# Second score pass of the later heads as 64-row products in the two halves of TensorE's rows

## The chip, the cores and the metric

The kernel runs on one core of a Trainium2 chip, as one program. The metric is the device time of one execution in microseconds (us), the median of several runs. Before the change it is 1375.22 us over 3 runs (1374.31 to 1378.02).

## The reference, cut to what matters

```python
scores = scale * np.matmul(q, k.transpose(0, 1, 3, 2))      # q, k, v: 4 x 12 x 448 x 64, f32
scores = cap * np.tanh(scores / cap)
scores = scores - np.max(scores, axis=-1, keepdims=True)
attn = np.exp(scores)
attn = attn / (np.sum(attn, axis=-1, keepdims=True) + 1e-09)
x = matmul(attn, v), heads side by side                      # 4 x 448 x 768
xn = (x - mu) / np.sqrt(var + 1e-06) * g_ln
x = x + np.maximum(xn @ w_ch1, 0.0) @ w_ch2                  # 768 -> 3072 -> 768
h = np.maximum(x.transpose(0, 2, 1) @ w_tok1, 0.0) @ w_tok2  # 448 -> 256 -> 448
u = x + h.transpose(0, 2, 1)
out = u + np.maximum(u @ w_ch1b, 0.0) @ w_ch2b               # 768 -> 1536 -> 768
```

Four batches, twelve heads each, head dimension 64. All inputs are f32.

## The kernel before, in words

**Data.** Activations lie transposed: channels on the 128 partitions, the 448 tokens along the free dimension. A product of TensorE here is one matmul instruction with a moving operand of 448 columns, and nearly all of them are made in fp32r, one pass over the columns. To keep f32 precision each operand x is split in two fp32r numbers: `high` is a rounded copy of x, `low` is x minus `high` (the helper `low`, L172, a subtraction). A product of two split operands is then made of high by high, high by low and low by high, the small low by low is left out (`PASSES`).

**Stages.** Batches 0 and 1 (`early`) come first: their attention works in plain f32, since TensorE has nothing else to do then. Their layer norm and the first MLP (`mlp`, L587 and L608, groups of four 128-wide hidden tiles), the token mixing (`tokens`) and the second MLP follow. The attention of batches 2 and 3 (the later heads, 24 of them) is woven in between the MLP products of batches 0 and 1. Then batches 2 and 3 go through the same MLPs and the token mixing, with no attention left to weave.

**Order of the work.** The program writes steps with `add(engine, cols, run, reads, writes, early)`; a step has a key (where in the program it belongs, minus `early`) and a cost, and `Program.emit` plays all steps through a list of engines: at each turn the engine that is free first takes the ready step with the lowest key. The instructions then stand on each engine in that fixed order. A step given as "dve+/pool+" goes to VectorE or GpSimd, whichever the planner finds free; steps marked + share one port in the planner, so that two of them do not overlap there. "act/dve*+" is a choice of ScalarE or VectorE.

**A later head.** Two DMAs bring q and k into `qk` and v into `v`. In `qk` the 64 rows of q and of k lie twice, in partitions 0 to 63 and again in 64 to 127 (`heads` in the launch code). Four steps prepare the scores: ScalarE writes `ks` (128x512), the high part of k in all 128 partitions (L347); a subtraction on GpSimd or VectorE overwrites partitions 64 to 127 of it with the low part (L348, recorded at L172), so that `ks` is [high; low]; and `qs` gets the high part of q in column block 0 and the low part in column block 1, both in all 128 partitions (L349, L350). There is one `ks` and one `qs` buffer, so they are written anew for a head when the scores of the head before are done.

The step `scores` (L358 to L366) makes for each half of a head two of its four blocks of 128 keys:

```python
for i in range(2):
    c, rows = 2 * half + i, slice(i * D, (i + 1) * D)
    ...
    for j in range(2):
        mm(sc.at[:, i, :S], ks.at[:, c * P:(c + 1) * P], qs.at[:, j], start=j == 0, stop=j == 1)
```

With j = 0 the 128 rows give (high k + low k) times high q, with j = 1 (high k + low k) times low q. So a half takes four products of 128 rows, a head eight, and the 24 later heads 192 in 48 halves. The two blocks of a half go to two PSUM banks (`sc.at[:, 0]` and `sc.at[:, 1]`).

The early heads (L363) take f32 operands: 64 rows of k and q, block i from the i-th half of the partitions. A product in f32 shows in the trace as two matmul records.

Behind the scores of a head stand tanh and exp on ScalarE (L369, L370), the row maxima and sums on VectorE (L374, L421), the split of the exponentials into `eh` and `el` (L394, L172, L400), the value products (L408) and the write into x (L429, L430).

Of the kernel before, what the change touches and what calls it, by code (L numbers as in the profile page):

```python
# [18 lines left out]
B, H, S, D = 4, 12, 448, 64  # L19
C = H * D  # L20
P = 128
# [38 lines left out]
URGENT, SCORES, PREPARE, LOAD = 1000.0, 19.31, 4.58, 24.58  # L60
# [26 lines left out]
class Program:  # L87
# [11 lines left out]
    def add(self, engine, cols, run, reads=(), writes=(), early=0.0):  # L99

        names = [(name.strip("*+"), "*" in name, "+" in name) for name in engine.split("/")]
        costs = {e: self.FIXED[e] + self.RATE[e] * cols * (0.5 if half else 1.0) for e, half, _ in names}
        step = Step(costs, run, (self.key - early, len(self.steps)))
        step.port = {e for e, _, port in names if port}
        before = set()
        for b in [p for b in reads for p in b.parts]:
            before.add(b.writer)
            b.readers.append(step)  # L110
        for b in [p for b in writes for p in b.parts]:
            before.add(b.writer)
            before.update(b.readers)
            b.writer, b.readers = step, []
        before -= {None, step}
        for s in before:
            s.users.append(step)
        step.waits = len(before)
        self.steps.append(step)
# [32 lines left out]
def block_kernel(ctx: ExitStack, tc: tile.TileContext, qkv, cap, gln, w1, w2, wt1, wt2, con, out):  # L152
    nc = tc.nc
    mm, act, dve = nc.tensor.matmul, nc.scalar.activation, nc.vector
    engine_of = {"dve": nc.vector, "pool": nc.gpsimd}
    prog = Program()
    add = prog.add
# [13 lines left out]
    def low(eng, out, whole, high):  # L171
        eng.tensor_tensor(out, whole, high.bitcast(F32), op=ALU.subtract)  # L172

    def copy(e, out, a):
        if e == "act":
            act(out, a, AF.Copy)  # L176
        else:
            dve.tensor_copy(out, a)
# [27 lines left out]
    def area(n):  # L206
        ends.append(ends[-1] + n)
        return area_t[:, ends[-2]:ends[-1]]
# [6 lines left out]
    two = [Box(area(S)), Box(area(S))]  # L215
# [113 lines left out]
    def attention(b, start, pace):  # L329
        x = x_t[b]  # L330
        early, beside = b < 2, b in BESIDE
# [5 lines left out]
        def head(h):  # L337
            grp = h // 6
            pr, hh = divmod(h, 2)
            qk, v, m = next(qks), next(vls), next(ms)  # L340
            add("dma", 480, lambda: nc.sync.dma_start(out=qk.at, in_=qkv[b, h, :, :S + 4 * P]), (), [qk], early=LOAD)
            add("dma", 192, lambda: nc.sync.dma_start(out=v.at, in_=qkv[b, h, :, S + 4 * P:].rearrange("p (c d) -> p c d", c=4)), (), [v], early=LOAD)
            q, k = qk.at[:, :S], qk.at[:, S:]
            if not early:

                (ks,), (qs,), (vs,), (eh,), (el,) = KS, QS, VS, EH, EL
                add("act", 4 * P, lambda: act(ks.at, k, AF.Copy), [qk], [ks], early=PREPARE)  # L347
                add("dve+/pool+", 4 * P, lambda e: low(engine_of[e], ks.at[D:], k[D:], ks.at[D:]), [qk], [ks], early=PREPARE)  # L348
                add("act/dve*+", S, lambda e: copy(e, qs.at[:, 0], q), [qk], [qs], early=PREPARE)  # L349
                add("dve+/pool+", S, lambda e: low(engine_of[e], qs.at[:, 1], q, qs.at[:, 0]), [qk], [qs], early=PREPARE)  # L350

            E = []
            for half in range(2):
                sc, eb = next(scs), next(es)
                e, eb = eb.at, [eb]
                E.append((e, eb))

                def scores(half=half, sc=sc):  # L358
                    for i in range(2):
                        c, rows = 2 * half + i, slice(i * D, (i + 1) * D)  # L360
                        if early:

                            mm(sc.at[:, i, :S], k[rows, c * P:(c + 1) * P], q[rows], start=True, stop=True)  # L363
                        else:
                            for j in range(2):
                                mm(sc.at[:, i, :S], ks.at[:, c * P:(c + 1) * P], qs.at[:, j], start=j == 0, stop=j == 1)  # L366

                add("pe", (6 if early else 4) * S, scores, [qk] if early else [ks, qs], [sc], early=URGENT + SCORES)
                add("act", 2 * S, lambda e=e, sc=sc: act(e, sc.at[:, :, :S], AF.Tanh, scale=tsc), [sc], eb)  # L369
                add("act", 2 * S, lambda e=e: act(e, e, AF.Exp, scale=cap_t), (), eb)  # L370

            for half in range(2):
                e, eb = E[half]
# [13 lines left out]
            else:  # L387
# [4 lines left out]
                for half in range(2):  # L392
                    e, eb = E[half]
# [23 lines left out]
            if beside:  # L417
                other, n = Box(E[1][0][:, 1], E[1][1]), next(sums)
                for half in range(2):
                    e, eb = E[half]  # L420
# [50 lines left out]
        for h in range(H):  # L471
            prog.key = start + h * pace
            head(h)
            if h % 6 == 5:
                prog.key = start + (h + 1) * pace
                divide(h // 6)
# [325 lines left out]
```

## Time and profile before

| | |
|---|---|
| median of 3 runs | 1375.22 us (1374.31 to 1378.02) |
| the profiled execution, first to last instruction (its span; nothing is recorded around it) | 4738.7 us |
| instructions in its trace | 17824, of them 6468 matmuls and 6468 weight loads |
| TensorE matmuls busy (PE) | 4729.0 us, 100% of the span |
| VectorE (DVE) busy | 897.2 us, 19% |
| ScalarE (ACT) busy | 624.6 us, 13% |
| GpSimd (POOL) busy | 88.9 us, 2% |
| DMA | 281.04 MB, 59 GB/s over the span |

The profiled execution took 3.45 times as long as the timed runs. So a duration of TensorE in the profile is not its duration in a timed run, and the shares of the other engines in the span are much smaller than their shares in a timed run must be. PE is TensorE's matmuls, PEld its weight loads, which may run beside matmuls. Line numbers such as L366 are those of the kernel before; the changed kernel's stand 3 or 4 higher behind the change.

### The profile page before, as it was taken

To read this page: it belongs to the slowest core of one execution; us is meant where nothing else is said; L and a number is where in the kernel's file an instruction comes from. 1 tells how busy PE (TensorE), PEld (TensorE's weight loads), DVE (VectorE), ACT (ScalarE), POOL (GpSimd) and SP (SyncE) were. 2 spreads that over 40 slices of the span, in tenths; PEclk is the share of its full clock that TensorE was granted. 3 is DMA by queue.
4 is the path that set the end of the run, shared out by engine and by line. 5 is a ranking of instruction groups with operands and counts; after the bars stand their busy time and mean duration, and the time that the engine had idled before them with its cause. 6 is when DMAs were issued, how large, how long until landed. Compare 5 with 4: busy or idle time off the path is not lost.

```text
span 4738.7 us, 17824 instructions
## 1 busy us (share of the span) xinstructions
PE 4729.0 (100%) x6468; PEld 2684.3 (57%) x6468; DVE 897.2 (19%) x1612; ACT 624.6 (13%) x1006; POOL 88.9 (2%) x79
## 2 busy tenths in 40 slices
PE   9999999999999999999999999999999999999999
PEld 2223555555655556665555555555656555656555
DVE  2231222222222222222222221100000000000000
ACT  3321111211121111121111110000000000000000
POOL 1100000000000000000000000000000000000000
DMA  3221122111212111221111211111111111111111
GB/s 105 97 66 39 46 69 67 59 61 64 67 55 67 63 57 41 67 65 61 60 60 51 72 57 53 57 62 58 53 53 44 61 59 60 51 47 42 37 57 58
DMA packets 147095, 281.04 MB, mean 59 GB/s; under 512 B 10816, under 2 KB 79680, under 8 KB 147008
## 3 DMA queue, kind: packets, MB, share of 16 engines
q1 hardware_dynamic: 146432, 279.62, 18.5%
q8 instruction: 51, 0.84, 0.1%
q10 hardware_dynamic: 576, 0.29, 0.0%
q14 instruction: 36, 0.29, 0.0%
HBM read 217.74 MB, written 62.13 MB: 59 GB/s over the span
## 4 chain that ended last, share of the span: by engine, by line
PE 100%; DMA 0%; ACT 0%; DVE 0%; issue 0%
PE bank L587 39%; PE bank L608 39%; PE bank L384 6%; PE sc L363 3%; PE sc L366 3%; PE bank L408 3%; PE bank L663 2%; PE bank L685 2%; PE bank L639 1%; PE bank L466 1%; PE bank L531 0%; PE bank L495 0%; PE bank L511 0%; DMA area<-in_qkv 0%; PE bank L445 0%; PE bank L444 0%
## 5 line engine op out<-in xcount | busy, mean ns | idle before, releaser
L587 PE MATMUL bank<-big,split 128*128 128x448 f32 x2592 | 1898.7, 995 | 1.1 <-ACT big L543 1.1
L608 PE MATMUL bank<-h,split 128*128 128x448 f32 x2592 | 1896.3, 995 | 0.0
L587 PEld LDWEIGHTS bank<-big,split 128*128 128x128 f32 x2592 | 1109.4, 429 | 750.5 <-issue 740.4
L608 PEld LDWEIGHTS bank<-h,split 128*128 128x128 f32 x2592 | 1109.5, 428 | 744.9 <-issue 741.6
L612 DVE TENSOR_TENSOR x<-x,bank 128x448 f32<-128x448 f32 x216 | 134.1, 621 | 1407.4 <-PE bank L608 1407.4
L592 ACT ACTIVATE h<-bank 128x448 fp32r<-128x448 f32 x144 | 78.4, 545 | 1817.5 <-PE bank L587 1817.5
L593 DVE SCALAR_TENSOR_TENSOR h<-bank,h 128x448 fp32r<-128x448 f32 x144 | 89.9, 624 | 1182.2 <-ACT h L592 1182.1
L366 PE MATMUL sc<-qs,ks 128*128 128x448 f32 x192 | 151.5, 994 | 0.0
L384 PE MATMUL bank<-x,area 128*96 128x448 f32 (+1 forms) x88 | 129.3, 1665 | 0.0
L363 PE MATMUL sc<-area 64*128 64x448 f32 x112 | 112.0, 1695 | 5.0 <-DMA area<-in_qkv 5.0
L366 PEld LDWEIGHTS sc<-qs,ks 128*128 128x128 f32 x192 | 82.5, 431 | 57.6 <-issue 57.2
L384 PE MATMUL bank<-x,x 128*96 128x448 f32 (+1 forms) x76 | 112.5, 1675 | 0.0
L685 PE MATMUL bank<-t,h 128*128 128x448 f32 x144 | 108.3, 996 | 0.0
L176 ACT ACTIVATE split<-whole 128x384 fp32r<-128x384 f32 (+1 forms) x96 | 54.0, 564 | 340.2 <-PE bank L608 228.7
L276 ACT ACTIVATE whole<-raw 128x384 f32<-128x384 f32 (+2 forms) x130 | 76.7, 593 | 125.5 <-DVE split L172 107.8
L663 PE MATMUL bank<-big,t 128*128 128x384 f32 x136 | 89.8, 899 | 0.0
L172 DVE TENSOR_TENSOR split<-whole,split 128x384 fp32r<-128x384 f32 (+1 forms) x112 | 68.9, 619 | 108.1 <-ACT split L176 107.7
L408 PE MATMUL bank<-el,vs 128*128 128x448 f32 x96 | 88.6, 989 | 0.0
L685 PEld LDWEIGHTS bank<-t,h 128*128 128x128 f32 x144 | 61.4, 427 | 40.8 <-issue 40.0
L384 PEld LDWEIGHTS bank<-x,area 128*96 128x96 f32 (+1 forms) x88 | 28.5, 347 | 95.4 <-issue 85.5
L279 DVE SCALAR_TENSOR_TENSOR whole<-raw,whole 128x384 int32<-128x384 int32 (+2 forms) x130 | 79.8, 616 | 0.2
L363 PE MATMUL sc<-x 64*128 64x448 f32 x80 | 79.4, 1692 | 0.0
(112 smaller groups left out, 1719.0 us busy)
## 6 DMA issues: line engine op xcount, KB each, us to landing
split<-kept SPq DMA_DIRECT2D x160, 384.0 KB, 3.4
split<-kept SPq DMA_DIRECT2D x120, 512.0 KB, 3.6
raw<-in_w SPq DMA_DIRECT2D x72, 384.0 KB, 3.3
kept<-split SPq DMA_DIRECT2D x72, 384.0 KB, 3.0
raw<-in_w SPq DMA_DIRECT2D x54, 512.0 KB, 3.6
kept<-split SPq DMA_DIRECT2D x54, 512.0 KB, 3.3
area<-in_qkv SPq DMA_DIRECT2D x38, 480.0 KB, 3.5
area<-in_qkv SPq DMA_DIRECT2D x35, 192.0 KB, 2.4
```

What stands on the lines that cost most here:

```text
L279: add("dve+", m, lambda: dve.scalar_tensor_tensor(f, hi, -(1 << 31), f, op0=ALU.bitwise_and, op1=ALU.bitwise_or), [r], [w])
L363: mm(sc.at[:, i, :S], k[rows, c * P:(c + 1) * P], q[rows], start=True, stop=True)
L366: mm(sc.at[:, i, :S], ks.at[:, c * P:(c + 1) * P], qs.at[:, j], start=j == 0, stop=j == 1)
L384: mm(po.at[:DV, :S], v.at[:n, c], E[c // 2][0][:n, c % 2], start=c == 0, stop=c == 3)
L408: mm(po.at[:, :S], vs.at[:, c, :P], part.at[:, i], start=c == 0 and part is eh, stop=c == 3)
L587: mm(ph.at[:, :S], w[:, wi, cc * P:(cc + 1) * P], src[cc].at[:, xi], start=(cc, n) == (0, 0), stop=(cc, n) == (NCC - 1, 2))
L592: add("act", S, lambda ht=ht, ph=ph: act(ht.at[:, 0], ph.at[:, :S], AF.Relu), [ph], [ht], early=EVACUATE)
L593: add("dve", S, lambda ht=ht, ph=ph: dve.scalar_tensor_tensor(ht.at[:, 1], ph.at[:, :S], 0.0, ht.at[:, 0].bitcast(F32), op0=ALU.max, op1=A ...
L608: mm(py.at[:, :S], w[:, wi, i * P:(i + 1) * P], h[i].at[:, hi], start=(i, n) == (0, 0), stop=(i, n) == (G - 1, 2))
L612: add("dve", S, lambda x=x, py=py: dve.tensor_tensor(x.at, x.at, py.at[:, :S], op=ALU.add), [py], [x], early=EVACUATE)
L663: mm(pj.at[:, :CC], t1[:, wi, sc * DT + j * P:sc * DT + (j + 1) * P], cols(xs[sc])[:, xi], start=(sc, wi, xi) == (0, 0, 0), stop=(sc, wi) ...
L685: mm(pu.at[:, :S], hT[j].at[:, hi, a:a + P], t2[:, wi, j * S:(j + 1) * S], start=(j, n) == (0, 0), stop=(j, n) == (1, 2))
```

## The change

For the later heads the low part of k is now laid out by key block. In the even blocks (0 and 2) it lies in partitions 64 to 127 as before, in the odd blocks (1 and 3) in partitions 0 to 63, and the high part in the other half. That takes two subtractions of 64 x (2x128) instead of one of 64x512. The first pass, all 128 rows of both blocks times high q, is unchanged in what it computes. The second pass takes only the 64 rows that hold high k, times the same 64 rows of low q: rows 0 to 63 for the half's first block, rows 64 to 127 for its second. The product low k by low q is thereby left out. The first pass of both blocks comes first, then the second pass of both. The planner's cost of a later half goes from 4 to 3 products of 448 columns.

```diff
@@ -345,7 +345,10 @@
 
                 (ks,), (qs,), (vs,), (eh,), (el,) = KS, QS, VS, EH, EL
                 add("act", 4 * P, lambda: act(ks.at, k, AF.Copy), [qk], [ks], early=PREPARE)
-                add("dve+/pool+", 4 * P, lambda e: low(engine_of[e], ks.at[D:], k[D:], ks.at[D:]), [qk], [ks], early=PREPARE)
+                for odd in range(2):
+                    lows = slice((1 - odd) * D, (2 - odd) * D)
+                    kl, kw = (t[lows].rearrange("p (a two c) -> p a two c", two=2, c=P)[:, :, odd] for t in (ks.at, k))
+                    add("dve+/pool+", 2 * P, lambda e, kl=kl, kw=kw: low(engine_of[e], kl, kw, kl), [qk], [ks], early=PREPARE)
                 add("act/dve*+", S, lambda e: copy(e, qs.at[:, 0], q), [qk], [qs], early=PREPARE)
                 add("dve+/pool+", S, lambda e: low(engine_of[e], qs.at[:, 1], q, qs.at[:, 0]), [qk], [qs], early=PREPARE)
 
@@ -356,16 +359,17 @@
                 E.append((e, eb))
 
                 def scores(half=half, sc=sc):
-                    for i in range(2):
-                        c, rows = 2 * half + i, slice(i * D, (i + 1) * D)
+                    blocks = [(i, slice((2 * half + i) * P, (2 * half + i + 1) * P), slice(i * D, (i + 1) * D)) for i in range(2)]
+                    if not early:
+                        for i, c, _ in blocks:
+                            mm(sc.at[:, i, :S], ks.at[:, c], qs.at[:, 0], start=True, stop=False)
+                    for i, c, rows in blocks:
                         if early:
-
-                            mm(sc.at[:, i, :S], k[rows, c * P:(c + 1) * P], q[rows], start=True, stop=True)
+                            mm(sc.at[:, i, :S], k[rows, c], q[rows], start=True, stop=True)
                         else:
-                            for j in range(2):
-                                mm(sc.at[:, i, :S], ks.at[:, c * P:(c + 1) * P], qs.at[:, j], start=j == 0, stop=j == 1)
-
-                add("pe", (6 if early else 4) * S, scores, [qk] if early else [ks, qs], [sc], early=URGENT + SCORES)
+                            mm(sc.at[:, i, :S], ks.at[rows, c], qs.at[rows, 1], start=False, stop=True)
+
+                add("pe", (6 if early else 3) * S, scores, [qk] if early else [ks, qs], [sc], early=URGENT + SCORES)
                 add("act", 2 * S, lambda e=e, sc=sc: act(e, sc.at[:, :, :S], AF.Tanh, scale=tsc), [sc], eb)
                 add("act", 2 * S, lambda e=e: act(e, e, AF.Exp, scale=cap_t), (), eb)
```

`sc` and the tiles are those of before, `P` is 128, `S` 448, `D` 64.

The order on TensorE (PE) at the first later head, batch 2's head 0, whose two halves write `sc_115` and `sc_116`; the neighbours are value products of the early heads. Before:

```order
L384 MATMUL bank_111<-x_82,x_83 96x448 x4
L366 MATMUL sc_115<-qs_95,ks_96 128x448 x4
L366 MATMUL sc_116<-qs_95,ks_96 128x448 x4
L384 MATMUL bank_112<-x_82,x_83 96x448 x2
L384 MATMUL bank_112<-x_83 96x448 x2
```

And now:

```order
L388 MATMUL bank_111<-x_82,x_83 96x448 x4
L365 MATMUL sc_115<-qs_95,ks_96 128x448 x2
L370 MATMUL sc_115<-qs_95,ks_96 128x448 x2
L365 MATMUL sc_116<-qs_95,ks_96 128x448 x2
L370 MATMUL sc_116<-qs_95,ks_96 128x448 x2
L388 MATMUL bank_112<-x_82,x_83 96x448 x2
L388 MATMUL bank_112<-x_83 96x448 x2
```

Each half's four products have become two of one line and two of another, with nothing between; here the halves stand at the same place.

The order on GpSimd (POOL) from its last weight subtraction on; `ks` is the low part of k, `qs` that of q. Before:

```order
L172 TENSOR_TENSOR split_79<-whole_75,split_79 128x512
L280 TENSOR_TENSOR whole_76<-whole_76,raw_73 128x512
L172 TENSOR_TENSOR split_77<-whole_76,split_77 128x512
L172 TENSOR_TENSOR ks_96<-area,ks_96 64x512
L172 TENSOR_TENSOR qs_95<-area,qs_95 128x448
```

And now:

```order
L172 TENSOR_TENSOR split_79<-whole_75,split_79 128x512
L280 TENSOR_TENSOR whole_76<-whole_76,raw_73 128x512
L172 TENSOR_TENSOR split_77<-whole_76,split_77 128x512
L172 TENSOR_TENSOR ks_96<-area,ks_96 64x2x128 x5
L172 TENSOR_TENSOR qs_95<-area,qs_95 128x448
```

Each subtraction on `ks` has become two. Counted over the whole listing, GpSimd has 46 of the 48 halves (22 of 24 whole ones before) and 22 of `qs` (23 before); VectorE has 2 halves of `ks` (2 whole ones before), 2 of `qs` (1 before), 2 casts of `qs` (4 before) and 40 casts of `split` (30 before), which ScalarE has lost. GpSimd goes from 84 to 107 instructions, VectorE from 1614 to 1623, ScalarE from 1012 to 1004; TensorE and the DMA issues keep their number.

The order on TensorE in the middle of batch 2's heads, where a group of the first MLP of batches 0 and 1 (`big_84` and `big_85`) begins: L587's products with weight buffers `split_77`, `split_78` and `split_79` follow one another. Before, from `split_78` on:

```order
L587 MATMUL bank_114<-big_84,split_78 128x448 x18
L587 MATMUL bank_112<-big_85,split_78 128x448 x6
L366 MATMUL sc_115<-qs_95,ks_96 128x448 x4
L408 MATMUL bank_111<-eh_98,vs_97 128x448
L408 MATMUL bank_111<-el_99,vs_97 128x448 x2
L587 MATMUL bank_112<-big_85,split_78 128x448 x12
L587 MATMUL bank_113<-big_84,split_79 128x448 x18
```

And now, from `split_77` on:

```order
L591 MATMUL bank_112<-big_84,split_77 128x448 x18
L365 MATMUL sc_116<-qs_95,ks_96 128x448 x2
L370 MATMUL sc_116<-qs_95,ks_96 128x448 x2
L591 MATMUL bank_113<-big_85,split_77 128x448 x18
L591 MATMUL bank_114<-big_84,split_78 128x448 x18
L591 MATMUL bank_112<-big_85,split_78 128x448 x18
L591 MATMUL bank_113<-big_84,split_79 128x448 x12
```

Inside the products with `split_78` stood the 21st of the 48 score halves; now none stands there, and ahead of them, among those with `split_77`, it is the 18th. Counted over the listing, the first two halves have 42 products of the MLPs and the token mixing ahead of them in both kernels, the 19th 1212 before and 1398 now, the 31st 2152 and 2278, the last 2908 and 2950.

## Rows read from the trace of the kernel before

**Rows 1.** The page: span, busy time by engine.
```profile
span 4738.7 us, 17824 instructions
...
PE 4729.0 (100%) x6468; PEld 2684.3 (57%) x6468; DVE 897.2 (19%) x1612; ACT 624.6 (13%) x1006; POOL 88.9 (2%) x79
```

**Rows 2.** Chain of waits, 3100 to 3300 us: start us, us, what, count.
```profile
3108.59 51.67 PE bank L608 x72
3160.25 51.82 PE bank L587 x72
```

**Rows 3.** Windows: us, busy (count) of PE, PEld, DVE, ACT, POOL, clock, DMA.
```profile
0.00:450.00 450.00, 445.04 (x445) 130.65 (x447) 119.49 (x207) 130.87 (x173) 32.51 (x34) 1.00 0.25 79
450.00:2850.00 2400.00, 2398.90 (x3365) 1425.29 (x3362) 619.14 (x1136) 428.15 (x710) 56.43 (x45) 1.00 0.19 60
450.00:4738.00 4288.00, 4283.93 (x6025) 2553.69 (x6021) 777.68 (x1406) 493.76 (x833) 56.43 (x45) 1.00 0.18 57
```

**Rows 4.** Groups by line: the later heads' score products.
```profile
L366 PE MATMUL sc<-qs,ks 128*128 128x448 f32 x192 | 151.5, 994 | 0.0
...
L366 PEld LDWEIGHTS sc<-qs,ks 128*128 128x128 f32 x192 | 82.5, 431 | 57.6 <-issue 57.2
```

**Rows 5.** Timeline, PE, switch from 128 to 64 rows: start us, us, what.
```profile
357.01 0.97 PE L587 MATMUL bank<-big,split 128*128 128x448 f32 x1
357.91 1.57 PE L363 MATMUL sc<-area 64*128 64x448 f32 x2
```

**Rows 6.** Timeline, PE, the next pair and the switch back.
```profile
359.32 1.63 PE L363 MATMUL sc<-area 64*128 64x448 f32 x2
360.88 0.91 PE L587 MATMUL bank<-big,split 128*128 128x448 f32 x1
```

**Rows 7.** Timeline, PE, the product after the switch back.
```profile
361.48 0.97 PE L587 MATMUL bank<-big,split 128*128 128x448 f32 x1
```

**Rows 8.** Timeline, PE, f32 records of 128 rows, one behind another.
```profile
472.16 6.04 PE L384 MATMUL bank<-x,x 128*96 128x448 f32 x4
477.88 1.79 PE L384 MATMUL bank<-x 128*96 128x448 f32 x1
```

**Rows 9.** Timeline, PEld, the weight loads around the switch.
```profile
356.20 0.46 PEld L587 LDWEIGHTS bank<-big,split 128*128 128x128 f32 x1 [0.18 <-DVE area L453]
357.91 0.23 PEld L363 LDWEIGHTS sc<-area 64*128 64x128 f32 x2 [1.25 <-issue]
```

**Rows 10.** Groups by line and shape: subtractions on POOL.
```profile
L172 POOL TENSOR_TENSOR ks<-area,ks 64x512 fp32r<-64x512 f32 x22 | 28.0, 1273 | 2350.3 <-ACT ks L347 2350.3
...
L172 POOL TENSOR_TENSOR split<-whole,split 128x384 fp32r<-128x384 f32 x8 | 8.0, 1005 | 44.1 <-ACT split L176 24.1 <-DVE split L178 20.0
...
L172 POOL TENSOR_TENSOR split<-whole,split 128x512 fp32r<-128x512 f32 x6 | 7.8, 1304 | 26.5 <-DVE split L178 17.4 <-ACT split L176 9.0
```

**Rows 11.** Groups by line and shape: steps on DVE that change.
```profile
L178 DVE CAST split<-whole 128x384 fp32r<-128x384 f32 x17 | 5.9, 350 | 3.2 <-PE bank L608 2.3 <-POOL whole L280 0.9
L178 DVE CAST split<-whole 128x512 fp32r<-128x512 f32 x13 | 5.5, 424 | 55.1 <-PE bank L608 40.5 <-PE bank L587 14.7
...
L178 DVE CAST qs<-area 128x448 fp32r<-128x448 f32 x4 | 1.5, 384 | 3.0 <-PE sc L366 3.0
...
L172 DVE TENSOR_TENSOR ks<-area,ks 64x512 fp32r<-64x512 f32 x2 | 1.4, 690 | 0.8 <-ACT ks L347 0.8
...
L172 DVE TENSOR_TENSOR qs<-area,qs 128x448 fp32r<-128x448 f32 x1 | 0.6, 626 | 0.0
```

**Rows 12.** The line of the later scores: idle before it, and who waited.
```profile
  ACT area L369: 0.4, 1
...
  ACT ks L347: 76.3, 14
  POOL qs L172: 17.5, 1
  DVE qs L178: 3.0, 1
  ACT area L369: 2.2, 1
```

## The prediction

> **What bounds the kernel now.** I read the page first, for the shares of the engines. TensorE's matmuls are busy 4729.0 us of the span of 4738.7 us, VectorE 897.2 us [rows 1]. So in the profiled execution TensorE ends everything, and the chain of waits runs through its lines alone. But that execution took 4738.7 us where the timed runs took 1375.22 (their median): the sum below is first made against the span and then carried over.
>
> How far a TensorE duration may be carried over is read from three views. In the chain, in a stretch of MLP products alone, 72 products of 448 columns follow one another in 51.67 us, 717.6 ns each [rows 2]. The windows show a granted clock of 1.00, the 2.4 GHz level, throughout [rows 3]; why the products are that far apart there, no row says. Counted in such products TensorE's 4729.0 us are 6590. Even if TensorE never waited in a timed run, a product can have taken no more than 1375.22 / 6590 = **208.7 ns**. The lower bound comes from the first 450 us of the profile, in which ScalarE is busy 130.87 us [rows 3]: at the overall ratio of 1375.22 / 4738.7 = 0.290 TensorE's part there would also be 130.6 us, so ScalarE and TensorE must alternate or overlap there; taken wholly one after the other they need 262 us. Then 1113 us are left for the 4283.93 us behind [rows 3], which are 5970 products: **186.5 ns** each. So TensorE's profile times shrink by a factor between 0.260 and 0.290.
>
> The times of the other engines do not shrink in that way: they have no part in TensorE's pace. That gives a second reading. From 450 to 2850 us, the stretch that holds the later heads, VectorE is busy 619.14 us of 2400 [rows 3]. In a timed run this stretch lasts about 2400 x 0.290 = 697 us, and VectorE then has 89% of it. TensorE is the bound there, but VectorE stands close behind.
>
> **What the change removes.** 48 halves of later heads make four products each, 192 in all [rows 4]. Now each half makes two full products and two of 64 rows. If the two 64-row products run beside each other in the two halves of the array, a half costs three products instead of four. The kernel already has such pairs, in f32, in the early heads: two 64-row records of L363 start at 357.91 (the row says x2), the next two both at 359.32, the product behind them at 360.88 [rows 5, 6]. One f32 record of 128 rows takes 5.72 / 4 = 1.43 us [rows 8], and a pair of 64 rows takes 1.41 to 1.56. So both halves really run at once. In fp32r no row shows a pair; I take it to do the same, since the f32 rows are the nearest. That removes 48 x 717.6 ns = 34.4 us of the profile.
>
> **What it adds on TensorE: two switches a half.** Between 128-row and 64-row products the engine does not go on seamlessly. The last full product before the pair starts at 357.01, the pair 0.90 us later instead of 0.72 [rows 5]; the pair's weight loads start with the pair, not under the product before, as the full products' loads do (356.20, 0.46 us long, under a running product) [rows 9]. From 357.01 to the second product behind the pair at 361.48 [rows 7] are 4.47 us. A product, two f32 records and a product would be 0.718 + 2 x 1.43 + 0.718 = 4.30. So going in and out costs 0.17 us, and 48 times that is 8.4 us of the profile. What is left is 34.4 - 8.4 = **26.1 us of the profile**, or a span of 4712.6 us.
>
> In the timed runs that is 26.1 x 0.260 to 0.290 = 6.8 to 7.6 us, if the switch shrinks as TensorE's other times do. I take that, because all that it consists of (the product running out, a weight load in the open) is TensorE's own work, and the middle, 7.2 us. The ends for the range: the switch costs nothing (48 x 186.5 to 208.7 ns = 9.0 to 10.0 us gained), or it keeps its 174 ns of the profile (48 x 12 to 35 ns = 0.6 to 1.7 us gained).
>
> Here rule and row differ. The Trainium skill (TensorE: Matmul & The Clock Gate, Measured speedup vs the span model) gives the span of concurrent row tiles as one matmul plus about 4 ns per further tile, and has no term for a switch; by it 48 pairs would give 48 x (208.7 - 4) ns = 9.8 us at most. The same skill (TensorEngine Tiling (Array Packing), Key Properties) says that changing the tiling mode drains the engine; the 0.90 us of [rows 5] agree. I go by the row.
>
> **What it moves on the other engines.** GpSimd gets 46 half subtractions for 22 whole ones. A half has 256 columns; the two subtractions of 384 and 512 columns took 1005 and 1304 ns [rows 10], 2.3 ns a column, so about 0.71 us (bounds: 0.64, half of a whole one's 1273, and 1.0). With one `qs` step less that is 46 x 0.71 - 22 x 1.27 - 1.24 = 3.5 us more, on an engine that is busy 56.43 us of 2400 [rows 3] and otherwise waits for ScalarE's `ks` (2350.3 us) [rows 10]: cost nothing. On a head's way to its scores it is 2 x 0.71 - 1.27 = 0.14 us more. What covers it: the scores' line waited 0.4 us in all, while `ks` and `qs` stood waiting for TensorE to be done with the head before [rows 12]. Without that cover it is 24 x 0.14 = 3.4 us.
>
> VectorE gets ten casts of weights that ScalarE had (6 x 350 + 4 x 424 ns), loses two of `qs` (384 each), gains one subtraction of `qs` (626), and two `ks` steps of 690 become two halves (345 to 690 each) [rows 11]: 3.0 to 3.7 us more. With 11% of the stretch free it costs nothing by itself; if VectorE is in truth the bound, it costs all of it.
>
> The score halves also move back, by up to 186 MLP products in the listing (the 19th), and come nearer to each other behind that. The heads' results are needed only by the MLP of batches 2 and 3, and the last half moves by 42 products, so nothing late is waited for; what it does to the queue on VectorE I cannot price beyond the case below.
>
> **Sum:** 1375.2 - 7.2 = **1368.0 us**.
>
> **The rivals.**
> 1. *The switch is free.* For it: the 64-row loads of the pair go side by side. Against it: the 0.90 us. Time 1375.2 - 9.0 to 10.0 = 1365.2 to 1366.2 us. The skill's span model above stands for this one.
> 2. *The switch does not shrink with TensorE's pace.* Then 0.6 to 1.7 us are gained: 1373.5 to 1374.6 us. No row can exclude it, since there is one pace in the trace.
> 3. *VectorE is the bound where the heads are.* Its 89% speak for it; that its instructions are spread by the planner, and that TensorE's line shows no wait, against. TensorE's gain turns into waits for VectorE and VectorE's extra work shows: 1375.2 to 1378.9 us.
> 4. *The two fp32r halves do not run at once.* Then the change does not do what it says: a half still takes four products and pays two switches. Place: L370, 48 times; price 174 ns x 0.260 = 45 ns to 174 ns, so 2.2 to 8.4 us: 1377.4 to 1383.6 us, slower. It decides as soon as the second product of a pair starts later than one product's time, less the switch, after the first. Only the missing fp32r row speaks for it; the f32 pairs speak against.
>
> **Chances.** The forecast 0.46, the free switch 0.08, the unshrunk switch 0.14, VectorE 0.18, serial halves 0.14. What a measurement of this kernel can tell from no change is about 0.3%, 4.1 us: below 1371.1 is faster, above 1379.3 slower. The first two cases lie below: 0.54. Rival 2, most of rival 3 and a third of rival 4 lie between: 0.34. The rest of rival 4 and a little of rival 3, where order waits come on top, is slower: 0.12. The range that holds the time 8 times in 10 goes from the free switch less the spread of the runs (0.9 us), and rounded down, 1364.0 us, to the end of rival 3 at 1378.5 us; the serial halves are mostly left out. The forecast alone would be 1366 to 1370.
>
> **What would show it.** In the profile of the changed kernel: 96 records of 64 rows on L370 that start two at a time; a span of about 4712.6 us; from the start of a half's last full product (L365) to that of the second product behind its pair 2.33 us, three products and 0.17. Wrong: the second of a pair starts a product later (rival 4); the span falls by 26 us but the timed median does not, and VectorE's casts stand ahead of TensorE's waits (rival 3); or the pairs cost far more than 0.17 us to enter and leave.

## The result, and the profile after

| | median | range | runs |
|---|---|---|---|
| before | 1374.76 us | 1370.12 to 1378.02 | 4 |
| changed | 1387.85 us | 1386.10 to 1388.34 | 4 |

The changed kernel is slower: ratio 1.0099, 95% interval 1.0076 to 1.0123, or 13.6 us of 1374.8 (the medians lie 13.1 us apart). The forecast was 1368.0 us, with 1378.5 as the upper end of its range.

The profile of the changed kernel was not slowed as that of the kernel before was: its span is 1386.2 us, that of a timed run. The page's first part and the row of the granted clock:

```profile
span 1386.2 us, 17870 instructions
...
PE 1362.6 (98%) x6468; PEld 1159.8 (84%) x6468; DVE 901.0 (65%) x1621; ACT 617.1 (45%) x998; POOL 100.1 (7%) x102
...
PEclk9999999999999999999999999999999999999999
```

So from here on TensorE's durations are those of timed runs. VectorE has 65% of the span (it had 19% of the slowed one [rows 1]), and its busy time has grown from 897.2 to 901.0 us.

Now the timeline of TensorE's matmuls at one half of a later head, and of its weight loads in the same place (start us, us, what; x2 are two that overlap; for the matmuls from three windows). They answer to the switch in [rows 5 to 7] and the loads in [rows 9]:

```profile
196.40 0.36 PE L365 MATMUL sc<-qs,ks 128*128 128x448 f32 x1
196.69 0.47 PE L370 MATMUL sc<-qs,ks 64*128 64x448 f32 x2
...
197.09 0.47 PE L591 MATMUL bank<-big,split 128*128 128x448 f32 x1
...
197.40 0.37 PE L591 MATMUL bank<-big,split 128*128 128x448 f32 x1
```

```profile
196.69 0.19 PEld L370 LDWEIGHTS sc<-qs,ks 64*128 64x128 f32 x2 [0.30 <-issue]
197.09 0.50 PEld L591 LDWEIGHTS bank<-big,split 128*128 128x128 f32 x3 [0.21 <-issue]
```

The two 64-row products of L370 start together at 196.69. But the step into them takes 0.29 us from the full product ahead, the pair 0.40 to the next full product, and that one 0.31 to its successor. The same view of the kernel before at the pace of a timed run (the first experiment below), matmuls and loads:

```profile
201.04 0.77 PE L587 MATMUL bank<-big,split 128*128 128x448 f32 x3
201.65 0.97 PE L366 MATMUL sc<-qs,ks 128*128 128x448 f32 x4
202.46 0.77 PE L587 MATMUL bank<-big,split 128*128 128x448 f32 x3
```

```profile
201.44 0.80 PEld L366 LDWEIGHTS sc<-qs,ks 128*128 128x128 f32 x4
202.26 0.80 PEld L587 LDWEIGHTS bank<-big,split 128*128 128x128 f32 x4
```

Four products of a half go through in 202.46 - 201.65 = 0.81 us, 203 ns each, and each load starts under the product ahead of its own. In the changed kernel it takes 1.00 us from the last full product (196.40) to the second product behind the pair (197.40), where three products would take 0.61: **the switch costs 0.39 us**, nearly two products, and the pair saves one. Over all 48 halves of this trace the same stretch takes 1.005 us in the median. Its parts can be seen in the load rows: the pair's load begins only with the pair (196.69), 0.29 us after the last full product, and the next full product's load begins only with that product (197.09). Each takes 0.18 to 0.19 us, and neither begins before the product ahead of it is nearly through (by the rows, whose ends are modelled, at 196.76 and 197.16). Two loads in the open are 0.37 of the 0.39 us; that they are the cause is argued here from the rows and tested below. Over 48 halves the loss is 48 x (0.39 - 0.203) = 9.0 us.

The switch that the prediction priced, between the MLP's products and the f32 pairs of the early heads [rows 5 to 7], stands in this trace too (matmuls, from five windows), and below it two f32 pairs of a longer block, with a third between them:

```profile
124.34 0.36 PE L591 MATMUL bank<-big,split 128*128 128x448 f32 x1
124.62 0.65 PE L368 MATMUL sc<-area 64*128 64x448 f32 x2
125.10 0.54 PE L368 MATMUL sc<-area 64*128 64x448 f32 x2
125.58 0.47 PE L591 MATMUL bank<-big,split 128*128 128x448 f32 x1
125.88 0.36 PE L591 MATMUL bank<-big,split 128*128 128x448 f32 x1
...
100.22 0.54 PE L368 MATMUL sc<-area 64*128 64x448 f32 x2
100.97 0.54 PE L368 MATMUL sc<-area 64*128 64x448 f32 x2
```

An f32 pair inside a block takes (100.97 - 100.22) / 2 = 0.375 us. From 124.34 to 125.88 are 1.54 us, where a product, two pairs and a product would take 1.16: at this pace that switch costs 0.38 us, where 0.17 was read from the slowed execution. So the price came out low through the pace, and not because the pairs there are f32.

That leaves 13.6 - 9.0 = 4.6 us for the rest of the change. The experiments separate the two.

### The profile page after: what moved, and what is told of

It reads as the page before. It is cut to its first block, busy times and chain, and to the rows that moved or that the text cites. A ratio compares the mean times of both kernels' runs of the same rounds, so it can differ in the third digit from the quotient of the medians.

```text
span 1386.2 us, 17870 instructions
## 1 busy us (share of the span) xinstructions
PE 1362.6 (98%) x6468; PEld 1159.8 (84%) x6468; DVE 901.0 (65%) x1621; ACT 617.1 (45%) x998; POOL 100.1 (7%) x102
## 4 chain that ended last, share of the span: by engine, by line
PE 90%; DVE 4%; ACT 4%; DMA 1%; issue 1%; ACTq 0%
PE bank L591 38%; PE bank L612 37%; PE bank L388 3%; PE bank L412 3%; PE bank L667 2%; PE bank L689 2%; PE sc L365 1%; PE sc L370 1%; ACT x L373 1%; PE sc L368 1%; ACT x L374 1%; DVE m L378 1%; PE bank L643 1%; DMA split<-kept 1%; PE bank L470 1%
## 5 line engine op out<-in xcount | busy, mean ns | idle before, releaser
L612 PE MATMUL bank<-h,split 128*128 128x448 f32 x2592 | 550.0, 368 | 3.5 <-DVE x L616 2.4
L591 PE MATMUL bank<-big,split 128*128 128x448 f32 x2592 | 548.9, 368 | 3.6 <-ACT big L547 1.8
L591 PEld LDWEIGHTS bank<-big,split 128*128 128x128 f32 x2592 | 483.4, 188 | 50.9 <-issue 6.5
L612 PEld LDWEIGHTS bank<-h,split 128*128 128x128 f32 x2592 | 483.3, 188 | 49.5 <-issue 6.0
L277 ACT ACTIVATE raw<-raw 128x384 int32<-128x384 uint32 (+2 forms) x130 | 77.6, 600 | 0.0
L280 DVE CUSTOM_DVE_ANT_0 whole<-raw,whole 128x768 uint16<-128x768 uint16 (+2 forms) x116 | 73.7, 637 | 0.0
L378 DVE TRANSPOSE_TENSOR_REDUCE m<-x 128x28 f32<-128x896 f32 x48 | 52.7, 1103 | 10.6 <-ACT x L374 10.1
L278 DVE TENSOR_SCALAR whole<-whole 128x384 int32<-128x384 int32 (+2 forms) x130 | 53.4, 413 | 3.6 <-ACT whole L276 3.2
L378 DVE TRANSPOSE_TENSOR_REDUCE m<-area 128x28 f32<-128x896 f32 x48 | 52.8, 1099 | 4.3 <-ACT area L374 4.3
L425 DVE TRANSPOSE_TENSOR_REDUCE n<-area 128x28 f32<-128x896 f32 x48 | 52.7, 1098 | 0.1
```

Of the source, the lines that this page charges most:

```text
L277: add("act", m, lambda: act(lo, lo.bitcast(U32), AF.Copy, scale=2.0 ** -29), (), [r])
L280: add("pool+" if ahead else "dve+", m, lambda e: engine_of[e].tensor_tensor(f, f, lo, op=ALU.add), [r], [w])
L378: add("dve", 2 * S, lambda half=half, e=e: dve.tensor_reduce(m.at[:, half].rearrange("p c j -> p (c j)"), e.rearrange("p c (j i) -> p (c j ...
L591: mm(ph.at[:, :S], w[:, wi, cc * P:(cc + 1) * P], src[cc].at[:, xi], start=(cc, n) == (0, 0), stop=(cc, n) == (NCC - 1, 2))
L612: mm(py.at[:, :S], w[:, wi, i * P:(i + 1) * P], h[i].at[:, hi], start=(i, n) == (0, 0), stop=(i, n) == (G - 1, 2))
```

## The experiments

The theory after the result, called "switch": each half pays two weight loads in the open. The rivals: "order", the moved heads and the other engines' extra work cost the time; and "VectorE is the bound where the heads are". The runs were timed in turn with the kernel before; ratios are to that, with their 95% intervals.

**The kernel before again**, no edit.

> The kernel before, unchanged, for a trace at the pace of the timed runs. All theories: the time of before, 1374.8 us within 0.3%. The profile of the changed kernel shows products of 448 columns 203 ns apart; here the four products of a half of the later scores should go through in 4 x 203 = 812 ns from the first to the next line's first, with no switch and all weight loads under running products. If instead a half takes over 1000 ns here too, the loss is not at the pairs.

Measured: 1373.71 us, ratio 0.9999 (0.9989 to 1.001), and the rows above: 0.81 us a half, all loads covered. What TensorE's and VectorE's shares are where the heads are woven in, these windows show (us, then busy time and count of PE, PEld, DVE, ACT, POOL, clock, DMA share, GB/s):

```profile
300.00:450.00 150.00, 150.00 (x741) 138.44 (x740) 139.83 (x256) 98.05 (x167) 13.66 (x10) 1.00 0.67 221
600.00:750.00 150.00, 150.00 (x747) 138.28 (x746) 137.06 (x255) 94.98 (x163) 14.62 (x10) 1.00 0.64 214
900.00:1050.00 150.00, 150.00 (x759) 139.27 (x758) 40.32 (x66) 19.49 (x37) 0.00 (x0) 1.00 0.58 190
```

VectorE has 91 to 93% of the two windows with heads, near the 89% that was worked out from [rows 3], while TensorE is busy throughout. Behind the heads, from 900 us on, it has 27%.

**The changed kernel with full products in the second pass:**

```diff
-                            mm(sc.at[:, i, :S], ks.at[rows, c], qs.at[rows, 1], start=False, stop=True)
+                            mm(sc.at[:, i, :S], ks.at[:, c], qs.at[:, 1], start=False, stop=True)
```

> The changed kernel, its order and its two subtractions on ks, but the second pass as two products of 128 rows, as before (it adds the product low k by low q again). Theory 'switch' (each half pays two weight loads in the open, 395 ns at entering and leaving the 64 rows, for 203 ns saved, so 48 x 0.19 = 9.4 us): the loss falls to what order and subtractions cost, 13.1 - 9.4 = 3.7 us, so about 1378.5 us (1376 to 1381). Rival 'order' (the moved heads and VectorE's extra work cost the time, the pairs nothing): it stays at 1388 us or above.

Measured: 1376.96 us, ratio 1.0030 (1.0017 to 1.0043), 4.1 us slower than before (2.3 to 5.9 by the interval). Two thirds of the loss are gone with the pairs. What is left comes with the order or the two subtractions.

**The pairs in the old order:** the two subtractions as one step of the planner, and

```diff
-                add("pe", (6 if early else 3) * S, scores, [qk] if early else [ks, qs], [sc], early=URGENT + SCORES)
+                add("pe", (6 if early else 4) * S, scores, [qk] if early else [ks, qs], [sc], early=URGENT + SCORES)
```

> The pairs of 64 rows alone: the two subtractions on ks are one step of the planner at the old cost and a half counts as four products there, so that every instruction on every engine stands where it stood before. Theory 'switch': 1374.8 + 9.4 = 1384.2 us (1382 to 1387), and the trace shows 290 to 298 ns into the pair, 400 for it and 309 behind it. Rival 'order': the pairs gain what was forecast, 1365 to 1370 us.

Measured: 1382.20 us, ratio 1.0066 (1.0049 to 1.0083), 9.1 us slower. TensorE's products stand in the same order in this trace as in that of the kernel before, so the pairs alone cost this. The two parts add up: 4.1 + 9.1 = 13.2 of 13.6 us. The rival "order" is out for the greater part, and so is any gain from the pairs.

**No second pass at all,** in the kernel before:

```diff
-                            for j in range(2):
-                                mm(sc.at[:, i, :S], ks.at[:, c * P:(c + 1) * P], qs.at[:, j], start=j == 0, stop=j == 1)
+                            for j in range(1):
+                                mm(sc.at[:, i, :S], ks.at[:, c * P:(c + 1) * P], qs.at[:, j], start=True, stop=True)
```

> The kernel before in its own order, but without the second pass of the later heads (high and low k by low q are left out): 96 products of 128 rows fewer, nothing else. It prices a product where the later heads stand. If TensorE is the bound there: 96 x 203 ns = 19.5 us less, 1355.3 us. Rival 'VectorE is the bound where the heads are': TensorE's gain turns into waits, 1368 to 1375 us. In between, the share gained says how much of a saved product counts.

Measured: 1356.06 us, ratio 0.9871 (0.9852 to 0.9890): 17.7 us less for 96 products fewer, 91% of the 19.5 us (78 to 104% by the interval). A product saved on TensorE counts nearly in full, although VectorE is over 90% busy there. "VectorE is the bound" is out.

**One 64-row block a head,** and the same steps with full products beside it. The scores of a head become one step:

```diff
+            def halves(both):
+                todo = [(sc, i, (2 * half + i) * P, slice(i * D, (i + 1) * D)) for half, sc in both for i in range(2)]
+                if not early:
+                    for sc, i, c, _ in todo:
+                        mm(sc.at[:, i, :S], ks.at[:, c:c + P], qs.at[:, 0], start=True, stop=False)
+                for sc, i, c, rows in todo:
...
+                        mm(sc.at[:, i, :S], ks.at[rows, c:c + P], qs.at[rows, 1], start=False, stop=True)
```

> One step of the planner makes all scores of a later head: first the four full products of both halves, then the four 64-row products as two pairs, one behind the other, so one switch in and out a head instead of two. Theory 'switch': the switch is paid once per block and the second pair's loads go under the first pair, so a head saves 2 x 203 ns and pays 395: 24 x 11 ns = 0.3 us gained over the same order with full products (the run beside it), that is the same time within the measurement. Rival 'each pair costs by itself' (the 64-row products are slow, not the change of rows): two pairs still lose 2 x 196 ns a head, 9.4 us more than the run beside it.

> The run that the one-block kernel is compared with: the same steps and the same order, but its second pass in products of 128 rows (low k by low q is added again). Both theories: near the time of before, 1374 us, plus or minus what the merged step does to the order (up to 5 us).

Measured: 1376.91 us, ratio 1.0019 (1.0008 to 1.0030), with the pairs; 1376.07 us, ratio 1.0013 (1.0003 to 1.0023), with full products. The difference, 0.06%, is within the measurement. So the same 96 products of 64 rows break even when they stand four together; what costs is the change of rows. The matmuls around such a block (from four windows) and its loads (start us, us, what):

```profile
201.42 0.36 PE L364 MATMUL sc<-qs,ks 128*128 128x448 f32 x1
201.71 0.47 PE L369 MATMUL sc<-qs,ks 64*128 64x448 f32 x2
...
202.02 0.36 PE L369 MATMUL sc<-qs,ks 64*128 64x448 f32 x2
202.31 0.47 PE L598 MATMUL bank<-big,split 128*128 128x448 f32 x1
...
202.62 0.36 PE L598 MATMUL bank<-big,split 128*128 128x448 f32 x1
```

```profile
201.70 0.30 PEld L369 LDWEIGHTS sc<-qs,ks 64*128 64x128 f32 x4 [0.30 <-issue]
202.30 0.30 PEld L598 LDWEIGHTS bank<-big,split 128*128 128x128 f32 x2 [0.30 <-DVE whole L278]
```

Four loads lie within 0.30 us from 201.70, so the second pair's run under the first pair; the next one in the open is that of the full product at 202.30. From 201.42 to 202.62 are 1.20 us, where four products would take 0.81: one switch of 0.39 us for the whole block, and two products (0.41 us) saved.

**Two switches a half:** each block's 64-row product directly behind its full one.

```diff
-                    if not early:
-                        for i, c, _ in blocks:
-                            mm(sc.at[:, i, :S], ks.at[:, c], qs.at[:, 0], start=True, stop=False)
                     for i, c, rows in blocks:
+                        if not early:
+                            mm(sc.at[:, i, :S], ks.at[:, c], qs.at[:, 0], start=True, stop=False)
```

> The changed kernel with a half's four products in another order: block 0 full, block 0 of 64 rows, block 1 full, block 1 of 64 rows. So no pair runs side by side and each half switches in and out twice. Theory 'switch': against the full products in the changed kernel's order (1377 us) nothing is saved and 2 x 395 ns are paid 48 times, 37.9 us: about 1415 us. If a switch did cost no more than the 0.17 us read from the slowed trace: 1377 + 48 x 0.35 = 1394 us.

Measured: 1415.85 us, ratio 1.0311 (1.0295 to 1.0326). Against the full products in the same order (1.0030) that is 2.81%, 38.6 us, where 37.9 were expected. The matmuls of one half:

```profile
200.82 0.37 PE L365 MATMUL sc<-qs,ks 128*128 128x448 f32 x1
201.11 0.47 PE L369 MATMUL sc<-qs,ks 64*128 64x448 f32 x1
201.51 0.47 PE L365 MATMUL sc<-qs,ks 128*128 128x448 f32 x1
201.91 0.47 PE L369 MATMUL sc<-qs,ks 64*128 64x448 f32 x1
```

The first change of the half takes 0.29 us, each further one 0.40, whether it goes to 64 rows or back. The loads in the same place:

```profile
201.11 0.18 PEld L369 LDWEIGHTS sc<-qs,ks 64*128 64x128 f32 x1 [0.31 <-issue]
201.51 0.19 PEld L365 LDWEIGHTS sc<-qs,ks 128*128 128x128 f32 x1 [0.22 <-issue]
201.91 0.18 PEld L369 LDWEIGHTS sc<-qs,ks 64*128 64x128 f32 x1 [0.21 <-issue]
```

At each change the load begins only with its own product.

**Narrow loads:** the 64-row products with 64 instead of 128 keys.

```diff
-                            mm(sc.at[:, i, :S], ks.at[rows, c], qs.at[rows, 1], start=False, stop=True)
+                            mm(sc.at[:D, i, :S], ks.at[rows, slice(c.start, c.start + D)], qs.at[rows, 1], start=True, stop=True)
```

> The changed kernel with weights of 64 instead of 128 keys in the 64-row products, which overwrite the upper half of a block's rows instead of adding to them: half of the second pass is left out. Theory 'loads in the open': the load ahead of the pair is shorter, and the pair's 400 ns to the next full product fall by as much as the load does, the 295 ns into the pair and the 309 behind it stay. Rival 'draining alone': the load's length plays no part and the 400 ns stay.

One run, 1384.4 us; the trace is what counts. The matmuls around one pair, from four windows, and the loads:

```profile
200.22 0.37 PE L365 MATMUL sc<-qs,ks 128*128 128x448 f32 x1
200.51 0.42 PE L370 MATMUL sc<-qs,ks 64*64 64x448 f32 x2
...
200.86 0.47 PE L591 MATMUL bank<-big,split 128*128 128x448 f32 x1
...
201.17 0.36 PE L591 MATMUL bank<-big,split 128*128 128x448 f32 x1
```

```profile
200.51 0.13 PEld L370 LDWEIGHTS sc<-qs,ks 64*64 64x64 f32 x2 [0.31 <-issue]
```

The pair now takes 200.86 - 200.51 = 0.35 us instead of 0.40, and its load 0.13 instead of 0.19. The pair became shorter by as much as its load, to the 10 ns that the rows give; the 0.29 us into the pair and the 0.31 behind it stayed. So the load does lie in the open, within the pair's time, and "draining alone" is out. That the load on the way back, 128 columns in all of these runs, lies in the open too is read from the load rows alone.

**What of the rest is order, what the second subtraction.** Two edits of the kernel before. The planner's cost alone:

```diff
-                add("pe", (6 if early else 4) * S, scores, [qk] if early else [ks, qs], [sc], early=URGENT + SCORES)
+                add("pe", (6 if early else 3) * S, scores, [qk] if early else [ks, qs], [sc], early=URGENT + SCORES)
```

> The kernel before with one number changed: the planner counts a later half as three products instead of four. All products are made as before; the order alone moves (the 19th score half gets 156 MLP products more ahead of it, as in the changed kernel). Theory 'moved order': this is the part of the loss that is not the switch, 1374 + 3.7 = about 1377.5 us. Rival 'the second subtraction' (the extra steps on GpSimd and VectorE cost it): 1374 us.

and the subtraction in two steps alone:

```diff
-                add("dve+/pool+", 4 * P, lambda e: low(engine_of[e], ks.at[D:], k[D:], ks.at[D:]), [qk], [ks], early=PREPARE)
+                for part in range(2):
+                    kl, kw = (t[D:, 2 * P * part:2 * P * (part + 1)] for t in (ks.at, k))
+                    add("dve+/pool+", 2 * P, lambda e, kl=kl, kw=kw: low(engine_of[e], kl, kw, kl), [qk], [ks], early=PREPARE)
```

> The kernel before with the subtraction on ks in two steps of 64x256, all else as before (products of 128 rows, the planner's cost 4). The heads hardly move in the order. Theory 'moved order': 1374 us, within 0.2%. Rival 'the second subtraction': about 1377.5 us.

Measured: 1384.32 us, ratio 1.0080 (1.0067 to 1.0093), for the planner's cost; 1372.81 us, ratio 0.9994 (0.9983 to 1.0004), for the two steps. The second subtraction costs nothing, as forecast. The order does cost, and how much depends on the order (counted in the traces, the 19th half has 186 more MLP products ahead of it in the changed kernel, 156 more with the planner's cost alone, 36 fewer with the two steps alone): the same number that comes with a loss of 4.1 us in the changed kernel's order (where the two steps shift the heads once more) costs 11 us alone, three times what I expected. What TensorE waited for from 160 to 1000 us (who, for whom, us in total, times, longest), first in the kernel before, then with the planner's cost alone:

```profile
PE bank L608 <- DVE x L612: 1.3, 1, 1.3
PE bank L587 <- ACT big L543: 1.1, 1, 1.1
PE bank L587 <- DVE big L172: 0.7, 1, 0.7
```

```profile
PE bank L608 <- DVE x L612: 5.6, 2, 3.2
PE sc L366 <- ACT area L369: 0.7, 1, 0.7
PE bank L587 <- DVE big L172: 0.4, 1, 0.4
PE bank L466 <- DVE el L172: 0.2, 1, 0.2
```

The longest is at 604 us. The timeline there, VectorE's part and then TensorE's product behind it:

```profile
601.64 0.69 DVE L279 SCALAR_TENSOR_TENSOR whole<-raw,whole 128x512 int32<-128x512 int32 x1
602.25 0.68 DVE L172 TENSOR_TENSOR split<-whole,split 128x512 fp32r<-128x512 f32 x1
602.85 0.69 DVE L280 CUSTOM_DVE_ANT_0 whole<-raw,whole 128x1024 uint16<-128x1024 uint16 x1
603.45 1.15 DVE L612 TENSOR_TENSOR x<-x,bank 128x448 f32<-128x448 f32 x2
```

```profile
604.12 0.47 PE L608 MATMUL bank<-h,split 128*128 128x448 f32 x1 [3.16 <-DVE x L612]
```

A product of L608 waited 3.16 us for a bank that VectorE's addition into x (L612) had to free; in VectorE's queue three steps of a weight conversion stood ahead of it. All waits of this view are 6.9 us, 3.8 more than before. The two profiled executions, both at a mean granted clock of 0.995, have spans of 1381.8 and 1372.0 us, 9.8 apart. So about 6 us of the cost stand in no wait of this view: they stay open.

## Why the prediction was wrong

- *TensorE bounds the kernel where the heads are.* Right: 91% of 96 products left out came back as time. A product took 203 ns, between the 186.5 and 208.7 worked out.
- *The two halves run at once in fp32r as in f32.* Right: both start at 196.69. Rival 4 is out.
- *48 products are saved.* Right, and by their spacing worth 48 x 203 ns = 9.7 us.
- *"So going in and out costs 0.17 us", with 0.174 us as the upper end.* **This step failed.** It costs 0.39 us. I read the cost as a difference of starts in a trace whose products were 718 ns apart; the same switch, around the same f32 pairs, costs 0.38 us at full pace. That in the slowed execution most of the open loads fell into slack around its products fits these numbers, but no run tests it. Then I let the difference shrink with the pace, or stay as it was, as the two ends. Neither end is one: what had to be carried over was the load itself. It stood in [rows 9], 0.23 us at the switch and in the open, and in the changed kernel's trace, at full pace, it is still 0.19. Two of them unshrunk, 0.46 us, less a product of at most 0.209, times 48 would have given 12 us slower. The load on the way back is in none of those rows; in the same trace it too begins with its product, at 360.88, and takes 0.22 us. Rival 2 named the mechanism ("does not shrink with TensorE's pace"), but its price was taken from the wrong rows.
- *The rule that I weighed.* The span model of the Trainium skill (TensorE: Matmul & The Clock Gate, Measured speedup vs the span model) agrees with the trace inside a block of 64-row products: both products of a pair start at 196.69, to the 10 ns of the rows. It has no term for the change of rows. The same skill says that changing the tiling mode drains the engine (TensorEngine Tiling (Array Packing), Key Properties). The rows agree as far as they go: a load that changes the rows begins 0.29 us after the last full product, while other loads begin under the product ahead. The price is this case's.
- *GpSimd's extra work costs nothing.* Right (0.9994 with the two steps alone); a half step took 849 ns on average in the changed kernel, where 710 were estimated within 640 to 1000:

```profile
L172 POOL TENSOR_TENSOR ks<-area,ks 64x256 fp32r<-64x256 f32 x46 | 39.0, 849 | 679.0 <-ACT ks L347 639.1 <-PE bank L612 39.2
```

- *VectorE gets 3.0 to 3.7 us more at no cost.* The size was right (897.9 in the kernel before at full pace, 901.0 changed: 3.1).
- *The moved heads, "I cannot price".* This term was put at nothing, and that failed too: the heads cost 4.1 us in this order (2.3 to 5.9), and 11 us in that of the planner's cost alone. It should have widened the range upward.

The sum with the measured terms: 1374.8 + 48 x (0.39 - 0.203) + 4.1 = 1387.9 us; measured 1387.85. With an interval of 3.6 us on the 4.1, agreement to 0.1 us is luck.

No version here that makes the second pass is faster than the kernel before beyond its interval. One block a head breaks even; a block of more would need more score banks than the two pairs that the kernel has, and was not tried.

## What to carry to other kernels

A block of 64-row products in a stream of 128-row products paid here for its way in and out with two weight loads that nothing hid, 0.39 us or 1.9 products of 448 columns; such a block has to save more than two of these products to be worth it. A cost that is read from an execution at another pace is carried over part by part: products shrank here from 718 to 203 ns, a load in the open only from 0.23 to 0.19 us, and the switch grew from 0.17 to 0.38. Where a planner sets the order, hold the order fixed in one run and change the order alone in another, since a single cost number moved this kernel by 0.8%.

## What the runs showed of the hardware

- In these traces loads of weights run under a product when both have the same rows, 128 or 64; where the rows change in the changed kernel, the load starts about 0.29 us after the last full product's start, a pair of 64 rows takes 0.40 us and the full product behind it 0.31, where 0.20 are usual.
- The loads of these products take 0.18 to 0.19 us for 128 columns, with 64 rows or 128, and 0.13 us for 64 columns with 64 rows. Columns alone do not set the time: the 72 loads of `kc` in the changed kernel (L643, also 128 x 128) take 0.14 us in the median. In the slowed execution, whose products were 3.5 times as far apart, a load in the open took 0.23 us.
- The slowed execution itself (718 ns a product at a granted clock of 1.00) did not come again in eleven further profiles; no row says what caused it.
